# Two layers of attention and feed-forward on one core: third score banks shared between the slots and VectorE, layer one opened in three parts, longer planned loads

## The chip, the cores and the metric

The kernel runs on one core of a Trainium2 chip. The metric is the device time of one execution in microseconds; for the kernel before it is the median of three runs. The profile is of one further execution and shows each engine: PE (TensorE, with its weight loads as PEld), ACT (ScalarE), DVE (VectorE), POOL (GpSimd) and SP, which here only issues transfers.

## The reference

The input is one sequence of 2048 positions with 512 features in bf16. Two equal layers follow one another, each an attention block and a feed-forward block with the same weights in both layers:

```python
def A(x, wqkv, wo):                    # 32 heads of 16
    q, k, v = split(x @ wqkv)
    p = softmax(q @ k.T * 16 ** -0.5)  # 2048 x 2048 for each head
    return (p @ v) @ wo
def B(x, w1, b1, w2, b2):              # 512 -> 1792 -> 512
    return gelu(x @ w1 + b1) @ w2 + b2
for _ in range(2):
    x = x + A(layernorm(x), wqkv, wo)
    x = x + B(layernorm(x), w1, b1, w2, b2)
```

The largest part by count is the exponential of the scores: 2 layers x 32 heads x 2048 x 2048 values.

## The kernel before

**Tiling.** The 2048 queries are cut into four chunks of 512 (the last chunk of layer one into two halves of 256), the keys into 16 tiles of 128, the heads into groups of 8 that share the 128 partitions. A *cell* is the score of one key tile against 512 columns of queries for one quarter of the partitions: a matmul of 32 rows (L1244) that fills one PSUM bank of 128 x 512 float32. There are 4096 cells. A *pass* is one layer, one query chunk, one group and a range of key tiles.

**Two ways to an exponential.** Most cells are read by ACT, which runs exp over two or three neighbouring banks in one instruction and writes bf16 (`exps`, L1601). The others go to DVE: it turns the bank into a 16-bit integer whose bits are an approximate exponential (`dfirst`, L1396), and three more copies of it, shifted by a constant, are made in pairs of cells, one by POOL (L1473), two by DVE (L1478, `dchain`). The value matmul (`pvs`, L1665) then uses one quarter-step for an ACT cell and four for a DVE cell, with scaled copies of V (`vcopies`, L1175), so that the four terms add up to a better exponential. Only the key tiles in `KD` can be DVE cells, five of 16 in each layer.

**Banks.** PSUM has eight banks. Banks 0, 1, 2 are slot 0 and banks 3, 4 slot 1; bank 6 collects the value matmul, of which four run side by side in four column quarters; banks 7 and 5 are `misc`, for projections and feed-forward. Once all first projections of layer zero are through, `grow` takes bank 5 for good and makes it the third bank of slot 1. A score step fills one slot. As it goes out, `swap` may give its third cell to DVE, if DVE is free within half a microsecond; then the slot comes back only when both ACT and DVE have read it (`slot_done`). `attach` may add DVE cells in a free bank of `misc`, and `solo` sends single ones while ACT has long work ahead.

**Parts.** A pass whose key tiles are only some of the 16 leaves its sums in SBUF: after the first part the bank is copied out (L818), and after the last one it is added (L830) and normalised (`norm`). Layer one begins with chunk 0 (8 groups) and half of chunk 1 (4 groups) over key tiles 0 to 11, and then the same 12 passes over tiles 12 to 15. The keys of layer one are ready chunk by chunk, as layer zero's feed-forward (`hpair`, `gelu`, `ytile`) and the projections (`proj`, L556 for all their matmuls) get done beside the attention.

**What sets the order.** All instructions of all engines are put in a fixed order before the launch by a list scheduler (`_Sched`): each operation has a planned cost, a planned latency after which its result counts as there, and a priority; `_Op("sp", cost, ..., tail=...)` is a transfer that holds SP's queue for `cost` and lands `tail` later. On the chip each engine works through its own list in order and waits on semaphores, so a transfer that takes longer than planned holds everything behind its first reader on that engine. Weights come in pieces of 256 KB through a ring of four buffers (`wload`, L933); normalised rows are transposed by DMA (`ln_tile`, L693).

The lines that the change touches most:

```python
SLOTS = ((0, 1, 2), (3, 4))
THIRD = 5
KD = ((4, 5, 6, 7, 8), (0, 1, 2, 12, 13))
...
out += run(1, s0, range(8), most, False, False) + run(1, s1, range(EARLY), most, False, False)
out += run(1, s0, range(8), rest, True, True) + run(1, s1, range(EARLY), rest, True, True)
...
yield _Op("sp", 0.37, lambda e: e.dma_start(dst, src), writes=["WR.%d" % w] + over, sem="dwr%d" % w, by=16, tail=2.48)
```

## Time and profile before

| | us |
|---|---|
| median of three runs (lowest, highest) | 1532.86 (1531.32, 1536.05) |
| profiled execution: its time | 1531.3 |
| profiled execution: its span | 1529.5 |
| ACT busy | 1477.3 |
| PE busy | 1441.2 |
| DVE busy | 1335.0 |
| POOL busy | 821.9 |

The span runs from the first to the last instruction. A row of a group gives the line in the code, the engine, the operation, what is written and read with the shapes, the count, the busy time, the mean duration of one, and the idle time just before them with what ended it. Busy time is counted once where instructions of a group overlap, so for ACT, whose instructions overlap a little, busy time divided by count is what one costs in a row of them. PE's matmuls are pipelined, and its busy time says less about how much more it could do. A row of the waits gives who waited for whom, the total, how often and the longest; PEld rows of that kind are weight loads that wait, often without holding PE.

### The profile page before, as it was taken

How to read it: one execution, taken by the hardware profiler on the slowest of the kernel's cores; microseconds unless marked ns; L12 is line 12 of the kernel's file. 1: busy time of each engine (PE TensorE's matmuls, PEld its weight loads, DVE VectorE, ACT ScalarE, POOL GpSimd, SP SyncE). 2: the span in 40 equal slices, each digit the busy share in tenths (PEclk: the TensorE clock that was granted, in tenths of full speed). 3: DMA queues.
4: the chain of work that ended last, by engine and by line, in shares of the span. 5: the costliest groups of instructions: out<-in, count | busy, mean ns of one | idle time of the engine just before them, and what ended most of it. 6: DMA issues, size and time to landing. Idle time of an engine off the chain costs nothing.

```text
span 1529.5 us, 46372 instructions
## 1 busy us (share of the span) xinstructions
PE 1441.2 (94%) x20257; PEld 441.6 (29%) x20257; DVE 1335.0 (87%) x2259; ACT 1477.3 (97%) x1369; POOL 821.9 (54%) x785
## 2 busy tenths in 40 slices
PE   8998899999999999999999999899999999999998
PEld 3222222222222222222222222222222222334345
DVE  6568889989998999978799778899989989999994
ACT  7999999999999999999999999999999999999995
POOL 5435546655564755545465455567555646464550
PEclk9999999999999999999999999999999999999999
DMA  5100001052111521126121441001143105311523
GB/s 155 41 2 1 2 12 40 29 174 77 48 31 53 144 83 36 43 64 166 50 56 38 130 133 29 1 2 36 37 151 93 43 23 170 109 36 33 167 69 98
DMA packets 145046, 103.40 MB, mean 68 GB/s; under 512 B 37069, under 2 KB 143822, under 8 KB 144846
## 3 DMA queue, kind: packets, MB, share of 16 engines
q1 hardware_dynamic: 144846, 100.44, 23.2%
q8 instruction: 162, 2.65, 0.7%
q14 instruction: 38, 0.31, 0.1%
HBM read 88.61 MB, written 4.19 MB: 61 GB/s over the span
## 4 chain that ended last, share of the span: by engine, by line
ACT 40%; PE 39%; DVE 14%; DMA 5%; POOL 1%; issue 1%; SPq 0%; DVEq 0%; ACTq 0%; POOLq 0%
ACT pt L1601 32%; PE ps L556 13%; PE ps L1665 13%; PE ps L1244 12%; DVE du L1396 6%; DVE du L1478 4%; DMA wr<-in_B_w_dram 2%; ACT kt L1601 2%; ACT q L1601 2%; ACT g L997 2%; DVE g L976 1%; ACT v L1601 1%; POOL xln L689 1%; DMA kt<-in_B_w_dram 1%; DMA xp<-xln 1%
## 5 line engine op out<-in xcount | busy, mean ns | idle before, releaser
L1601 ACT ACTIVATE pt<-ps 128x1024 bf16<-128x1024 f32 (+1 forms) x1112 | 1198.2, 1218 | 19.1 <-PE ps L1244 13.3
L1473 POOL TENSOR_SCALAR du<-du 128x1024 uint16<-128x1024 uint16 (+1 forms) x479 | 562.2, 1175 | 495.6 <-DVE du L1396 481.2
L1396 DVE TENSOR_SCALAR du<-ps 128x512 uint16<-128x512 f32 x956 | 634.9, 680 | 93.5 <-PE ps L1244 88.6
L1244 PE MATMUL ps<-qp,kt 32*128 32x512 bf16 x4096 | 530.0, 384 | 37.3 <-ACT pt L1601 20.7
L1665 PE MATMUL ps<-pt,v 128*17 128x512 bf16 (+1 forms) x2876 | 407.3, 360 | 11.4 <-ACT pt L1601 6.3
L1665 PE MATMUL ps<-du,vc 128*17 128x512 bf16 (+1 forms) x3228 | 384.3, 357 | 3.5 <-ACT pt L1601 1.8
L1478 DVE TENSOR_SCALAR du<-du 128x2048 uint16<-128x2048 uint16 (+1 forms) x479 | 351.4, 743 | 10.7 <-POOL du L1473 10.6
L1244 PEld LDWEIGHTS ps<-qp,kt 32*128 32x128 bf16 x4096 | 137.2, 91 | 581.6 <-ACT pt L1601 214.1
L1665 PE MATMUL ps<-du,v 128*17 128x512 bf16 (+1 forms) x1076 | 178.7, 358 | 10.3 <-ACT pt L1601 3.3
L1673 PE MATMUL ps<-vc,zero 128*17 128x512 bf16 x919 | 182.5, 381 | 0.0
L556 PE MATMUL ps<-xf,wr 128*32 128x512 bf16 (+1 forms) x1888 | 129.5, 364 | 4.2 <-DMA xf<-xln 2.0
L1665 PEld LDWEIGHTS ps<-pt,v 128*17 128x17 bf16 x2876 | 99.2, 88 | 108.0 <-issue 65.2
L1665 PEld LDWEIGHTS ps<-du,vc 128*17 128x17 bf16 x3228 | 100.2, 89 | 89.5 <-issue 54.8
L556 PE MATMUL ps<-wr,g 128*32 128x512 bf16 x1600 | 117.6, 384 | 7.6 <-DMA wr<-in_B_w_dram 6.4
L1192 POOL TENSOR_SCALAR qp<-q,mask 128x512 bf16<-128x512 bf16 (+1 forms) x91 | 71.1, 781 | 76.6 <-PE ps L1244 69.9
L1601 ACT ACTIVATE kt<-ps 128x1536 bf16<-128x1536 f32 (+1 forms) x77 | 98.9, 1294 | 2.9 <-PE ps L1244 1.2
L976 DVE TENSOR_SCALAR g<-ps,hb1t 128x512 bf16<-128x512 f32 (+1 forms) x112 | 78.4, 703 | 6.0 <-PE ps L556 5.4
L1473 POOL TENSOR_SCALAR kt<-kt 128x1024 uint16<-128x1024 uint16 (+1 forms) x46 | 53.4, 1161 | 46.9 <-DVE kt L1396 46.8
L1601 ACT ACTIVATE v<-ps 128x1024 bf16<-128x1024 f32 (+1 forms) x69 | 73.9, 1139 | 2.0 <-PE ps L1244 1.2
L1396 DVE TENSOR_SCALAR kt<-ps 128x512 uint16<-128x512 f32 x91 | 62.0, 681 | 7.3 <-PE ps L1244 5.6
L1665 PE MATMUL ps<-kt,v 128*17 128x512 bf16 (+1 forms) x309 | 67.5, 365 | 0.3 <-ACT pt L1601 0.2
L1665 PEld LDWEIGHTS ps<-du,v 128*17 128x17 bf16 x1076 | 45.1, 88 | 63.3 <-issue 25.7
(90 smaller groups left out, 1234.0 us busy)
## 6 DMA issues: line engine op xcount, KB each, us to landing
wr<-in_B_w_dram SPq DMA_DIRECT2D x256, 256.0 KB, 2.9
wr<-in_A_wqkv_dram SPq DMA_DIRECT2D x24, 256.0 KB, 3.0
wr<-in_A_wo_dram SPq DMA_DIRECT2D x18, 256.0 KB, 3.6
x<-in_A_x_dram SPq DMA_DIRECT2D x7, 512.0 KB, 4.1
kept<-x SPq DMA_DIRECT2D x4, 512.0 KB, 2.9
x<-kept SPq DMA_DIRECT2D x4, 512.0 KB, 3.9
out_dram<-x SPq DMA_DIRECT2D x16, 128.0 KB, 2.4
g<-in_A_wqkv_dram SPq DMA_DIRECT2D x3, 512.0 KB, 5.1
```

The costliest lines, as they stand in the source:

```text
L556: return [lambda e, a=a: e.matmul(out[32 * a:32 * a + 32, :], lhsT=lhsT[:, 32 * a:32 * a + 32], rhs=rhs, start=start, stop=stop, tile_posi ...
L689: yield _Op(eng, cost, lambda e: e.tensor_scalar(T["XLN"][:, x, :], T["X"][:, t % XT, :], T["RSTD"][:, t:t + 1], T["NMR"][:, t:t + 1], op0 ...
L976: yield _Op("dve", 0.21 + n / 966, lambda e, fc=fc, pb=pb: e.tensor_scalar(T["G"][:, fc, q], pb, T["HB1T"][:, fc:fc + 1], None, op0=ALU.ad ...
L997: lambda e, g=g: e.activation(out=g, in_=g, func=ACT.Gelu_apprx_tanh), reads=gk, writes=gk, prio=2)
L1192: yield _Op("pool", 0.27 + 0.42 * w / 512, lambda e, s=s, q=q, i=i, t=t, w=w: e.tensor_scalar(T["QP"][:, s, w * i:w * i + w], q, T["MASK"] ...
L1244: return (lambda e: e.matmul(o, lhsT=lhsT, rhs=rhs, start=True, stop=True, tile_position=(32 * a, 0)), ["K%d.%d.%d" % (l, gb, kt // 4), "Q ...
L1396: yield _Op("dve", 0.682, lambda e: e.tensor_scalar(u, self.bank(b), E_SCALE, E_BIAS, op0=ALU.mult, op1=ALU.add), reads=["B.%d" % b], writ ...
L1473: one = _Op("pool", 0.15 + 0.45 * n, lambda e, a=a, b=b: e.tensor_scalar(b, a, float(SHIFT), 1.0, op0=ALU.add, op1=ALU.mult), reads=key[0] ...
L1478: two = _Op("dve", 0.152 + 0.266 * n, lambda e: e.tensor_scalar(U[:, 2:4, 0:n, :], U[:, 0:2, 0:n, :], 2 * SHIFT, None, op0=ALU.add), reads ...
L1601: yield _Op("act", 0.065 + 0.4267 * n, lambda e, src=src, dst=dst: e.activation(out=dst, in_=src, func=ACT.Exp, scale=0.25), reads=["B.%d" ...
L1665: op.fns.append(lambda e, o=o, lhsT=q[0][0][m], rhs=q[0][1][:, n * m:n * m + n], a=a, st=st, sp=sp: e.matmul(o, lhsT=lhsT, rhs=rhs, start= ...
L1673: op.fns.append(lambda e, o=self.bank(b)[32 * a:32 * a + 17, :], rhs=rhs, a=a, st=not begun[a], sp=end: e.matmul(o, lhsT=T["ZERO"][:, 0:17 ...
```

## The change

- Each slot keeps two banks of its own, 0 and 1, and 3 and 4. Banks 2 and 5 are the slots' thirds and lie in the pool for DVE's cells (`dbank`) while nobody uses them. `grow`, `swap` and `slot_done` go. As a score step goes out, `attach` may put DVE cells into whatever banks are free, the first if DVE is free within half a microsecond, each further one if it is free 0.6 us earlier; if it attached none, `extend` lets ACT's exp take the slot's own third bank, if that is free by then. A slot comes back as soon as ACT has read it. Bank 5 can go to `misc` when more than four operations wait for a bank there, or more than one after the third query chunk of layer one.
- Layer one opens with key tiles 0 to 7, then 8 to 11, then 12 to 15, over the same 12 groups. The middle part is added to the sums in SBUF by DVE. DVE's key tiles in layer one become 0, 1, 2, 8 and 12.
- Planned costs of transfers: weight loads 1.5 and 2.5 in place of 0.37 and 2.48, moves 1.5 and 4.0 in place of 0.42 and 3.7, transposes 0.3 and 3.5 in place of 1.2 and 1.35, stores 1.0 in place of 0.42.
- Smaller ones: the key buffer of chunk 1 of layer one is lent to exp results as those of chunks 3 and 2 are; DVE's reading of a bank goes ahead of its exponent cells where it isn't one; the value matmul goes out with fewer quarters when two (not one) DVE buffers are left; which buffers an instruction is told to wait for is narrowed in three places and widened for the lent ones.

```diff
-SLOTS = ((0, 1, 2), (3, 4))
+SLOTS = ((0, 1), (3, 4))
 PVB = 6
 MISC = (7, 5)
-THIRD = 5
+THIRD = (2, 5)
 PT_RING = 15
-LEND = (3, 2)
+LEND = (3, 2, 1)
...
+DCELL = 0.6
+PARTS = (8, 12)
+KD = ((4, 5, 6, 7, 8), (0, 1, 2, 8, 12))
...
+SEVAC = 0.2
-RUSH = 4
+RUSH = 1
...
-DULOW = 1
+DULOW = 2
...
-LATENCY = {"pe": 0.219, "act": 0.21, "dve": 0.139, "pool": 0.153328, "sp": 0.1}
+LATENCY = {"pe": 0.2185, "act": 0.21, "dve": 0.139, "pool": 0.153328, "sp": 0.1}
...
-                        item.prio = min(th.prio, EVAC)
+                        item.prio = min(th.prio, EVAC if item.writes[0].startswith("DU") else SEVAC)
...
     def xmove(self, c, src, dst, sem, reads, writes):
-        yield _Op("sp", 0.42, lambda e: e.dma_start(dst, src), reads=reads, writes=writes, sem=sem, by=16, tail=3.7)
+        yield _Op("sp", 1.5, lambda e: e.dma_start(dst, src), reads=reads, writes=writes, sem=sem, by=16, tail=4.0)
...
-            yield _Op("sp", 1.2, lambda e: e.dma_start(dst(t), T["XLN"][:, x, :], transpose=True),
-                      reads=["XLN.%d" % x], writes=dkeys(t), sem="dtr%d" % x, by=16, tail=1.35)
+            yield _Op("sp", 0.3, lambda e: e.dma_start(dst(t), T["XLN"][:, x, :], transpose=True),
+                      reads=["XLN.%d" % x], writes=dkeys(t), sem="dtr%d" % x, by=16, tail=3.5)
...
                     yield ("need", ("k1", c))
+                    keys += self.lentkeys(LEND.index(c))
...
-                      writes=["Q.%d.%d" % (i, c)])
+                      writes=["Q.%d.%d" % (i, c)] + (self.lentkeys(len(LEND) + c) if l else []))
...
         if not final:
-            yield _Op("dve", DV, lambda e: e.tensor_copy(pt, pv), reads=[key], writes=[pk] + over)
+            if part:
+                yield _Op("dve", DV, lambda e: e.tensor_tensor(out=pt, in0=pt, in1=pv, op=ALU.add), reads=[key, pk], writes=[pk])
+            else:
+                yield _Op("dve", DV, lambda e: e.tensor_copy(pt, pv), reads=[key], writes=[pk] + over)
...
     def wload(self, piece, src, n, uses, w, over):
         dst = self.T["WR"][w].rearrange("p (c f) -> p c f", c=n)
-        yield _Op("sp", 0.37, lambda e: e.dma_start(dst, src), writes=["WR.%d" % w] + over, sem="dwr%d" % w, by=16, tail=2.48)
+        yield _Op("sp", 1.5, lambda e: e.dma_start(dst, src), writes=["WR.%d" % w] + over, sem="dwr%d" % w, by=16, tail=2.5)
...
-            yield _Op("sp", 0.42, lambda e: e.dma_start(self.hbm["out"][:, t, :], T["X"][:, t % XT, :]), reads=["X.%d" % (t % XT)],
+            yield _Op("sp", 1.0, lambda e: e.dma_start(self.hbm["out"][:, t, :], T["X"][:, t % XT, :]), reads=["X.%d" % (t % XT)],
...
-        every, most, rest = range(NT), range(NT - 4), range(NT - 4, NT)
+        every, parts = range(NT), [range(a, b) for a, b in zip((0,) + PARTS, PARTS + (NT,))]
         self.segs = [[(c, 0, 512) for c in range(self.NQ)] for _ in range(NL)]
         self.segs[-1][-1:] = [(self.NQ - 1, 0, 256), (self.NQ - 1, 256, 256)]
         s0, s1 = self.segs[1][:2]
         out = run(0, s0, range(8), range(4), False, False) + run(0, s0, range(8), range(4, NT), True, True)
         for seg in self.segs[0][1:]:
             out += run(0, seg, range(8), every, False, True)
-        out += run(1, s0, range(8), most, False, False) + run(1, s1, range(EARLY), most, False, False)
-        out += run(1, s0, range(8), rest, True, True) + run(1, s1, range(EARLY), rest, True, True)
+        for i, kts in enumerate(parts):
+            for seg, n in ((s0, 8), (s1, EARLY)):
+                out += run(1, seg, range(n), kts, i > 0, i == len(parts) - 1)
...
+        if b == THIRD[0]:
+            return "misc" if self.ended else "dbank"
         q = self.s.waiting("misc")
         if self.lend == 2:
             return "misc"
...
+        self.fresh = set()
         self.lead = [min(pi for pi, p in enumerate(self.pas) if p[0] == l) for l in range(NL)]
         self.slots = [list(x) for x in SLOTS]
-        self.held, self.users = [len(x) for x in SLOTS], [0] * len(SLOTS)
+        self.held, self.thirds = [len(x) for x in SLOTS], list(THIRD)
         self.dmine = {c for q in self.dlist for c in q}
...
-    def join(self, op, d, b, extra, free):
+    def join(self, op, d, b, extra, free, merge=False):
...
-        if op.fns and not self.third(b):
+        if op.fns and not merge:
             op.after.append(_Op("pe", MM, f, reads=r, writes=["B.%d" % b], mode="S"))
         else:
             op.fns.append(f)
...
-    def swap(self, op, start, cells, extra, free, sl):
-        if extra or self.lend == 2 or len(cells) < 3 or not (self.open or self.s.pools["du"]):
+    def banked(self, b, start):
+        return all(self.s.end.get(ev, 0.0) <= start for ev in self.P.deps([], ["B.%d" % b]) if ev[0] != "pe")
+
+    def extend(self, op, start, cells, extra, free, sl):
+        b, tok = self.thirds[sl], self.s.tokens
+        if extra or len(cells) < 2 or b not in self.s.pools["dbank"] or not self.banked(b, start):
             return
-        if self.s.clock["dve"] > start + SWAP:
+        pa, c = self.pa, self.next_act()
+        if c is None:
             return
-        c = cells[-1]
-        if c in self.dmine:
+        l, seg, g = self.pas[c[0]][:3]
+        need = [("qp", c[0]), ("K", l, self.heads(seg, g)[0], c[1] // 4)]
+        r = []
+        if c[2] not in {x[2] for x in cells} and all(k in tok for k in need):
+            f, r = self.score(c, tok[need[0]], b)
+        if not r or self.s.landed(r) > start:
+            (self.dlist if c in self.dmine else self.alist)[c[0]].insert(0, c)
+            self.pa = pa
             return
-        d = self.next_d({x[2] for x in cells[:-1]}, start)
-        if d is None:
-            return
-        cells.pop()
-        f, r = self.score(c, self.s.tokens[("qp", c[0])], self.slots[sl][2])
-        op.fns.pop()
-        op.writes.pop()
-        self.scored -= 1
-        self.left[c[0]] += 1
-        if self.left[c[0]] == 1:
-            free.remove(self.s.tokens[("qp", c[0])])
-        self.pa = min(self.pa, c[0])
-        self.alist[c[0]].insert(0, c)
-        self.join(op, d, self.slots[sl][2], extra, free)
+        self.s.pools["dbank"].remove(b)
+        cells.append(c)
+        op.fns.append(f)
+        op.reads += r
+        op.writes.append("B.%d" % b)
+        self.take(c, free)
 
...
+                if b in self.thirds and self.s.clock["dve"] + DCELL * len(extra) > start + SWAP:
+                    continue
...
-                self.join(op, d, b, extra, free)
+                self.join(op, d, b, extra, free, self.banked(b, start))
...
-            op.late = lambda op, start, sl=sl, cells=cells, extra=extra, free=free: (self.attach(op, start, cells, extra, free), self.swap(op, start, cells, extra, free, sl))
+            op.late = lambda op, start, sl=sl, cells=cells, extra=extra, free=free: (self.attach(op, start, cells, extra, free), self.extend(op, start, cells, extra, free, sl))
...
-        if not self.third(b):
-            yield ("rel", "dbank", b)
-        else:
-            yield from self.slot_done(self.third(b) - 1)
+        yield ("rel", "dbank", b)
...
-    def third(self, b):
-        return sum(i + 1 for i, x in enumerate(self.slots) if b in x)
-
-    def grow(self):
-        for c in range(self.NQ):
-            for kind in "KVQ":
-                for i in range(4):
-                    yield ("need", (kind, 0, 4 * c + i if kind == "V" else i, c))
-        for home in ("dbank",):
-            yield ("cond", lambda: THIRD in self.s.pools["dbank"] or THIRD in self.s.pools["misc"])
-            home = "dbank" if THIRD in self.s.pools["dbank"] else "misc"
-            yield ("take", (home, THIRD))
-        self.slots[1].append(THIRD)
-
-    def slot_done(self, sl):
-        self.users[sl] -= 1
-        if self.users[sl] == 0:
-            yield ("rel", "s", sl)
-
     def over(self, du):
-        return ["K0.%d.%d" % (i, c) for i in (2, 3) for c in range(self.NQ)] if du == len(self.cap) - 1 else []
+        if du not in self.fresh:
+            return []
+        self.fresh.remove(du)
+        return ["K0.%d.%d" % (i, c) for i in (2, 3) for c in range(self.NQ)]
 
     def morebuf(self):
...
+    def lentkeys(self, b):
+        return ["PT.%d" % u for u in range(*self.blocks[1 + b])]
+
...
-                  writes=["W2.%d" % c] + ["Q.%d.%d" % (i, c) for i in range(NDC)], sem="dw%d" % c, by=16, tail=2.5)
+                  writes=["W2.%d" % c] + ["Q.%d.%d" % (i, c) for i in range(NDC)] + self.lentkeys(len(LEND) + c), sem="dw%d" % c, by=16, tail=2.5)
...
-                reads=["B.%d" % b for b in self.slots[sl][:n]], writes=[k for r in run for k in self.pkeys(r)])
+                reads=["B.%d" % b for b in (self.slots[sl] + self.thirds[sl:sl + 1])[:n]], writes=[k for r in run for k in self.pkeys(r)])
...
-                                         ["V%d.%d" % (l, kt), "V%d1" % l] + self.pkeys(r), ("pt", r), True, kt))
-            yield from self.slot_done(sl)
+                                         ["V%d.%d" % (l, kt), "V%d1" % l, "PT.%d" % r], ("pt", r), True, kt))
+            yield ("rel", "s", sl)
+            if n > 2:
+                yield ("rel", "dbank", self.thirds[sl])
...
-        s.pool("dbank", [])
+        s.pool("dbank", THIRD[:1])
...
-        s.spawn(self.grow(), 0)
```

3 lines of the change are left out of this document (1 added, 2 removed).

## The prediction

> **What bounds the kernel now.** I read the page's engine totals first, then the groups with shapes kept apart, then the windows by stage, the waits, and the load lines one by one.
>
> ```profile
> span 1529.5 us, 46372 instructions
> PE 1441.2 (94%) x20257; PEld 441.6 (29%) x20257; DVE 1335.0 (87%) x2259; ACT 1477.3 (97%) x1369; POOL 821.9 (54%) x785
> ACT 40%; PE 39%; DVE 14%; DMA 5%; POOL 1%; issue 1%; SPq 0%; DVEq 0%; ACTq 0%; POOLq 0%
> ```
>
> ACT is occupied 97% of the span, so only 1529.5 - 1477.3 = 52.2 us can come from filling its gaps; anything more has to take work off ACT. The chain is shared by ACT and PE, so PE cannot be loaded freely either. DVE has the most room: 1529.5 - 1335.0 = 194.5 us idle.
>
> ```profile
> L1601 ACT ACTIVATE pt<-ps 128x1024 bf16<-128x1024 f32 x753 | 735.9, 1072 | 16.1 <-PE ps L1244 12.6 <-PE ps L1665 2.1
> L1601 ACT ACTIVATE pt<-ps 128x1536 bf16<-128x1536 f32 x358 | 511.6, 1526 | 3.0 <-PE ps L1665 1.4 <-PE ps L1244 0.7 <-PE ps L1673 0.6
> L1244 PE MATMUL ps<-qp,kt 32*128 32x512 bf16 x4096 | 530.0, 384 | 37.3 <-ACT pt L1601 20.7 <-DVE du L1396 4.9 <-ACT kt L1601 2.4
> L1396 DVE TENSOR_SCALAR du<-ps 128x512 uint16<-128x512 f32 x956 | 634.9, 680 | 93.5 <-PE ps L1244 88.6
> L1396 DVE TENSOR_SCALAR kt<-ps 128x512 uint16<-128x512 f32 x91 | 62.0, 681 | 7.3 <-PE ps L1244 5.6
> L1478 DVE TENSOR_SCALAR du<-du 128x2048 uint16<-128x2048 uint16 x477 | 350.6, 744 | 10.7 <-POOL du L1473 10.6
> L997 ACT ACTIVATE g<-g 128x3584 bf16<-128x3584 bf16 x14 | 43.9, 3182 | 0.1
> ```
>
> The exp line by itself, one row for each buffer that it writes:
>
> ```profile
> L1601 ACT ACTIVATE pt<-ps x1112: 591/1092/1775, 13.2 to 1499.2; 128x1024 bf16<-128x1024 f32 x116, 128x1536 bf16<-128x1536 f32 x70
> L1601 ACT ACTIVATE kt<-ps x77: 1017/1445/1720, 88.7 to 893.5; 128x1536 bf16<-128x1536 f32 x40, 128x1024 bf16<-128x1024 f32 x37
> L1601 ACT ACTIVATE v<-ps x69: 1017/1069/1520, 1044.0 to 1497.8; 128x1024 bf16<-128x1024 f32 x55, 128x1536 bf16<-128x1536 f32 x14
> L1601 ACT ACTIVATE q<-ps x52: 1017/1112/1633, 261.5 to 1315.8; 128x1024 bf16<-128x1024 f32 x34, 128x1536 bf16<-128x1536 f32 x18
> ```
>
> A cell is one score bank of 512 columns. There are 4096; DVE takes 956 + 91 = 1047 and ACT the other 3049, in 1112 + 77 + 69 + 52 = 1310 exps (the last four rows). Prices from these rows: by busy time divided by count, a two-bank exp occupies ACT for 735.9/753 = 0.977 us and a three-bank one for 511.6/358 = 1.429, so the third bank costs 0.45 us and an instruction as such 0.977 - 2 x 0.452 = 0.073. A cell on DVE costs 0.68 + 0.744/2 = 1.05 us there. So each cell that DVE takes in addition is worth 0.45 us of ACT, and each three-bank exp that falls apart costs 0.073 per instruction more.
>
> **The change, part by part.** First, the third banks. Today banks 2 and 5 belong to their slot: when DVE takes the third cell, the slot is not given back until DVE has read it, and at most one cell per step is swapped to DVE. While ACT runs a gelu (two in a row of 3.2 us in most stages), the slots are full and only bank 7 is left for single DVE cells. The windows of the exponent line on DVE show it, in pairs of a stage before a gelu and the stage with it:
>
> ```profile
> 450.00:475.00 25.00, 13.72 (x22) 1.00 0.11 33
> 475.00:500.00 25.00, 9.86 (x16) 1.00 0.28 85
> 650.00:675.00 25.00, 13.71 (x21) 1.00 0.14 39
> 675.00:700.00 25.00, 6.87 (x10) 0.93 0.45 140
> 825.00:850.00 25.00, 11.99 (x18) 1.00 0.11 33
> 850.00:875.00 25.00, 9.98 (x15) 1.00 0.49 149
> 1075.00:1100.00 25.00, 13.39 (x21) 1.00 0.12 33
> 1100.00:1125.00 25.00, 9.76 (x15) 1.00 0.28 87
> 1375.00:1400.00 25.00, 12.92 (x20) 1.00 0.12 34
> 1400.00:1425.00 25.00, 10.83 (x18) 1.00 0.38 115
> ```
>
> (Columns: stage, its length, DVE busy with that line and how many, granted clock, DMA share, GB/s.) The gelu stages lack 6 + 11 + 3 + 6 + 2 = 28 cells. After the change banks 2 and 5 may be lying free for DVE during a gelu, or may hold a third ACT cell, as it falls; I take half: 14 x 0.45 = **-6.3 us**. The bounds are 0 and 28 x 0.45 = 12.6.
>
> Outside the gelus DVE still waits for scores: 88.6 + 5.6 = 94.2 us in the rows above. The 28 missing cells account for 28 x 1.05 = 29 of it, which leaves 65. An idle DVE can now be given two cells in one step, and a slot need not wait for DVE. I take a third, 22 us, which is 21 cells, 21 x 0.45 = -9.4 us; the bound is 65/1.05 x 0.45 = 28. Against it stands that a third bank used by DVE is missing to its slot's next step, whichever slot the DVE cell came with; then a step carries two cells. How often PE today finds DVE in its way:
>
> ```profile
> PEld ps L1244 <- DVE du L1396: 118.0, 265, 1.3
> ```
>
> In 265 cases a score step waits for a bank that DVE holds. If one in three goes out two wide instead, ACT gets 88 more instructions: 88 x 0.073 = +6.4 us; all 265 would be 19. PE gets 88 more steps; 530.0 us over 1310 steps is 0.40 us a step, so 36 us, covered by PE's 1529.5 - 1441.2 = 88 us idle. If that cover is gone, they cost up to 36. Net of this part **-3.0 us**, between -28 and +19. The Trainium skill, page "ScalarE: Activation LUTs", section "What ACT_TABLE_LOAD costs", speaks against this step more than my row: it gives an ACTIVATE with immediates 186 ns beside its elements, of which about 93 overlap with its neighbour, so 93 ns a piece. By it the 88 instructions would cost an estimated 8.2 us, and the whole forecast would be 1.8 us later.
>
> Second, the loads. The plan counted a weight load as 0.37 us of the queue and 2.48 to landing, and now counts 1.5 and 2.5; moves, transposes and stores are stretched too. The load line itself, the waits on it over the whole run, and ACT's two gaps in the worst stage:
>
> ```profile
> L933 SPq DMA_DIRECT2D wr<-in_B_w_dram x256: 367/368/1429, 10.1 to 1506.8; - x128
> DMA to landing us min/median/max: 2.5/3.0/5.9
> PEld ps L556 <- DMA wr<-in_B_w_dram: 12.0, 19, 1.4
> PE ps L556 <- DMA wr<-in_B_w_dram: 6.4, 8, 1.1
> 687.97 1.02 ACT L1601 ACTIVATE pt<-ps 128x1024 bf16<-128x1024 f32 x1 [0.84 <-PE ps L1244]
> 689.91 1.02 ACT L1601 ACTIVATE pt<-ps 128x1024 bf16<-128x1024 f32 x1 [0.92 <-PE ps L1244]
> ```
>
> Issue goes from 0.37 to 1.43 us, and landing to 5.9, so the old figure is the best case and the new one near the worst. PE runs a fixed order: a late weight holds the scores behind it, and ACT and DVE after them. PE waits 12.0 + 6.4 = 18.4 us on these weights. In the stage 675 to 700 ACT lost 0.84 + 0.92 = 1.8 us behind it. Between 0 and 18.4 I take **-3.4 us**, two such stages, since most waits are short and ACT has one slot in hand. Nothing is issued more often; SP's queue keeps the same loads (256 in the row above), and only the matmuls that use them are put later. A chunk's 28 second-layer loads planned 1.13 us slower each end 32 us later at most; that is hidden while nothing downstream is due, and would cost up to 32 us where it is.
>
> Third, layer one opens with key tiles 0-7, then 8-11, then 12-15, so chunk 2 of its keys is due 192 cells later than now. ACT's gaps around that opening, and the prices of one more part:
>
> ```profile
> 745.06 5.13 ACT L1601 ACTIVATE pt<-ps 128x1024 bf16<-128x1024 f32 x5 [0.66 <-PE ps L1244]
> 757.26 2.79 ACT L1601 ACTIVATE pt<-ps 128x1536 bf16<-128x1536 f32 x2 [0.71 <-PE ps L1244]
> 791.85 6.46 ACT L1601 ACTIVATE pt<-ps 128x1024 bf16<-128x1024 f32 x6 [1.88 <-PE ps L1665]
> 866.31 2.14 ACT L1601 ACTIVATE kt<-ps 128x1024 bf16<-128x1024 f32 x2 [0.70 <-PE ps L1244]
> L830 DVE TENSOR_TENSOR v<-v,ps x16: 670/677/689, 98.9 to 1023.0; 128x512 f32<-128x512 f32 x16
> L1192 POOL TENSOR_SCALAR qp<-q,mask 128x512 bf16<-128x512 bf16 x75 | 60.7, 809 | 67.3 <-PE ps L1244 61.0 <-ACT q L756 5.7
> PE ps L1665 <- DVE v L830: 3.7, 10, 0.8
> ```
>
> The four gaps are 0.66 + 0.71 + 1.88 + 0.70 = 4.0 us; I take 2.7 back (bounds 0 and 4.0). Twelve more passes mean 12 additions on DVE, 12 x 0.677 = 8.1 us, or 7.7 cells not taken, 3.5 us of ACT if DVE were full; it is not in this stretch, so half, +1.7. They mean 12 x 0.81 = 9.7 us on POOL, queued between its shifts for DVE, covered by POOL's 46% idle; without that cover each would delay a DVE pair by 0.8. Each boundary also keeps the single accumulator bank from PE for about 0.37 us (3.7/10), 4.4 us under PE's idle time, or all of it on the path. Net **-1.0 us**, from -4.0 to +8.
>
> The rest I put at 0 together, with ends of -3 and +5. Evacuations ahead of DVE's cells free bank 7 sooner and make a DVE cell wait one instruction of 0.68. Lending bank 5 to the projections (over four waiters, over one near the end) narrows slot 1 meanwhile. Four more tile units for exps help a ring on which ACT shows no wait; the key evacuations and the late weight load that now also wait for these units come long after the units were read. Offering vectors at two free buffers sends out emptier accumulation steps, on PE's idle time. The last 30 us, after the final exp, run as before.
>
> Sum: -6.3 - 3.0 - 3.4 - 1.0 = **-13.7 us**. The profiled execution took 1531.3 us (span 1529.5); it lies 1.6 under the median 1532.86 of the three runs. Applied to the median it gives **1519 us**.
>
> **The rivals.** (A) Two-cell steps make PE the bound, slower than before. DVE picks the third bank that has been free longest, so a cell of slot 1's step can sit in bank 2, and both slots then lose a third in turn. For it: the chain gives PE 39%, and some stages have no PE room at all:
>
> ```profile
> 1150.00:1175.00 25.00, 25.00 (x334) 6.82 (x330) 24.64 (x42) 25.00 (x27) 15.18 (x14) 1.00 0.35 106
> 1175.00:1200.00 25.00, 22.93 (x307) 6.31 (x304) 23.19 (x42) 25.00 (x22) 17.00 (x16) 1.00 0.19 44
> ```
>
> (Here PE, weight load, DVE, ACT and POOL.) Against: the stage beside it has 2 us of room in 25. From about 88/0.40 = 220 extra steps PE's idle time is used up; at 250, with half of them in full stages, 125 x 0.40 = 50 us are added, less the 6.3 + 3.4 = 9.7 us of the gelu stages and the loads, which makes about 1573 (ACT's 250 x 0.073 = 18 us lie beside it). Milder, at 150 steps with a third exposed, 20 - 9.7 = +10, **1543**, which I take as this rival's time. (B) The plan only shifts: DVE takes as many cells as now, and the loads' -3.4 is all that is left beside the boundaries' +1.7: **1531**. For it: DVE's own supply, 5 of 16 key tiles, is not raised. (C) The longer planned loads put the feed-forward work off into the layer's opening, where the 32 us above are due at once: half exposed, 16, less the banks' 6.3 + 3.0, makes +6.7: **1540**. Against: the same opening is relaxed by 192 cells.
>
> **How the numbers follow.** Forecast (1504 to 1527) 0.67, A 0.13, B 0.10, C 0.10. A measurement of this kernel tells about 0.3%, 4.6 us, from no change: its three runs span 1531.32 to 1536.05. B lies within it; A and C are slower. So faster 0.67, same 0.10, slower 0.23. The likeliest case's own range goes from -29, a little under half of what all gains' bounds give together (12.6 + 28 + 18.4 + 4.0 + 3 = 66; ACT, PE and DVE cannot all be relieved at once), to -6, where the floating banks cost 3 outside the gelus in place of gaining 3 and the loads give half: 1504 to 1527. For 8 in 10 I leave out the far ends of A and of the gains: 1503 to 1547.
>
> **What would show it.** DVE's exponent line should count 1070 to 1100 cells instead of 1047, with the gelu stages at 15 or more; two-bank exps some 90 up; PE's waits on weights below 10 us; 12 additions more and ACT's gaps around the opening under 2 us; ACT busy near 1465. It would be wrong if the exps rise by 150 or more with DVE's count unchanged (A), if DVE's count stays within 10 (B), or if ACT shows gaps of microseconds where layer one opens (C).

## The result and the profile after

| | before | after |
|---|---|---|
| median (lowest, highest), four runs each | 1534.45 (1531.32, 1537.68) | 1513.76 (1513.23, 1514.69) |
| profiled execution (one of the four): its time | 1531.3 | 1514.7 |
| its span | 1529.5 | 1512.9 |
| ACT busy, and idle in the span | 1477.3, 52.2 | 1475.2, 37.7 |

The ratio is 0.9866, with a 95% interval from 0.9842 to 0.9889: the change made the kernel faster by 1.3%, 20.7 us by these medians and 16.6 by the two profiled executions. (Why these two differ is told under the clock, below.) The forecast was 1519.

The engine totals and the head of the chain of waits of the changed kernel:

```profile
span 1512.9 us, 46350 instructions
PE 1455.4 (96%) x20161; PEld 439.5 (29%) x20161; DVE 1364.8 (90%) x2295; ACT 1475.2 (98%) x1433; POOL 844.0 (56%) x811
ACT 55%; PE 29%; DVE 13%; DMA 1%; POOL 1%; issue 1%; ACTq 0%
```

The split of the gain stands in the first two lines. The span is 16.6 us shorter, but ACT is busy only 2.1 us less; the other 14.5 us are gaps of ACT that closed. In the chain ACT's share rose from 40% to 55%, and DMA's fell from 5% to 1%. Next, the groups of ACT whose gaps changed, with all shapes of a buffer in one row (the last columns are busy time and mean, then the idle time before them and its releasers); first the kernel before:

```profile
L1601 ACT ACTIVATE pt<-ps 128x1024 bf16<-128x1024 f32 (+1 forms) x1112 | 1198.2, 1218 | 19.1 <-PE ps L1244 13.3 <-PE ps L1665 3.6 <-PE ps L1673 0.6
L1601 ACT ACTIVATE kt<-ps 128x1536 bf16<-128x1536 f32 (+1 forms) x77 | 98.9, 1294 | 2.9 <-PE ps L1244 1.2 <-PE ps L1665 0.8
L1601 ACT ACTIVATE v<-ps 128x1024 bf16<-128x1024 f32 (+1 forms) x69 | 73.9, 1139 | 2.0 <-PE ps L1244 1.2 <-PE ps L1673 0.2
L1601 ACT ACTIVATE q<-ps 128x1024 bf16<-128x1024 f32 (+1 forms) x52 | 61.3, 1206 | 0.8 <-PE ps L1244 0.6
L971 ACT ACTIVATE g<-ps,hb1t 128x256 bf16<-128x256 f32 x14 | 6.0, 474 | 4.3 <-PE ps L556 4.3
```

and the kernel after:

```profile
L1601 ACT ACTIVATE pt<-ps 128x1024 bf16<-128x1024 f32 (+1 forms) x1111 | 1144.3, 1160 | 8.3 <-PE ps L1667 5.0 <-PE ps L1255 2.4
L1601 ACT ACTIVATE kt<-ps 128x1024 bf16<-128x1024 f32 (+1 forms) x126 | 145.4, 1178 | 3.1 <-PE ps L1255 1.3
L1601 ACT ACTIVATE v<-ps 128x1024 bf16<-128x1024 f32 (+1 forms) x89 | 97.3, 1143 | 1.0
L1601 ACT ACTIVATE q<-ps 128x1024 bf16<-128x1024 f32 (+1 forms) x48 | 56.0, 1213 | 0.4 <-PE ps L1255 0.3
L978 ACT ACTIVATE g<-ps,hb1t 128x256 bf16<-128x256 f32 x14 | 6.0, 473 | 1.2 <-PE ps L559 1.2
```

The exps waited 19.1 + 2.9 + 2.0 + 0.8 = 24.8 us before and 8.3 + 3.1 + 1.0 + 0.4 = 12.8 after; the waits for scores (L1244, now L1255) fell from 16.3 to 4.0 us (13.3 + 1.2 + 1.2 + 0.6 against 2.4 + 1.3 + 0.3). The small gelus near the end, which read a bank directly (L971, now L978), gave 3.1 more. The counts say how the work changed: 1111 + 126 + 89 + 48 = 1374 exps in place of 1310, so 64 more instructions. The main buffer's exps by shape:

```profile
L1601 ACT ACTIVATE pt<-ps 128x1024 bf16<-128x1024 f32 x883 | 852.7, 1073 | 2.1 <-PE ps L1255 1.4
L1601 ACT ACTIVATE pt<-ps 128x1536 bf16<-128x1536 f32 x228 | 328.3, 1499 | 6.2 <-PE ps L1667 5.0 <-PE ps L1255 1.1
```

They were 753 and 358 before. Over all four buffers two-bank exps rose from 879 to 1083, and three-bank ones fell from 430 to 291. And the lines of DVE that matter, by shape (L1411 was L1396, L1475 was L1478; L823 is the new addition, which has 4 more in another buffer):

```profile
L1411 DVE TENSOR_SCALAR du<-ps 128x512 uint16<-128x512 f32 x967 | 632.9, 682 | 61.8 <-PE ps L1255 57.7
L1411 DVE TENSOR_SCALAR kt<-ps 128x512 uint16<-128x512 f32 x90 | 59.8, 682 | 5.6 <-PE ps L1255 5.5
L1475 DVE TENSOR_SCALAR du<-du 128x2048 uint16<-128x2048 uint16 x475 | 358.4, 769 | 8.3 <-POOL du L1470 8.2
L1475 DVE TENSOR_SCALAR du<-du 128x1024 uint16<-128x1024 uint16 x17 | 8.5, 511 | 0.5 <-POOL du L1470 0.5
L823 DVE TENSOR_TENSOR v<-v,ps 128x512 f32<-128x512 f32 x8 | 5.4, 680 | 0.2 <-PE ps L1667 0.2
```

DVE takes 967 + 90 = 1057 cells, only 10 more than before. At 0.45 us that is 4.5 us less for ACT, and 64 instructions at 0.073 are 4.7 more: ACT's work is nearly the same, as its busy time says. DVE's waits for scores did fall, from 94.2 to 57.7 + 5.5 = 63.2 us, but the freed time did not go into cells. DVE is busy 1364.8 - 1335.0 = 29.8 us more, and half of that is the copies of a DVE cell in this buffer: 358.4 + 8.5 us, where the kernel before has 350.6 for 477 long ones and 0.8 for two short ones. There are two fewer long copies, but each takes longer (769 ns in place of 744), and 15 more short ones. Why the long ones take longer no run shows. With the twelve new additions (12 x 0.68 = 8.2) that is some 23 us.

The stages of the gelus, 20 us each from the table load ahead of the pair, DVE's exponent line alone (length, busy and count, granted clock, DMA share, GB/s); before:

```profile
299.16:319.16 20.00, 9.89 (x15) 1.00 0.47 145
484.56:504.56 20.00, 8.41 (x13) 1.00 0.43 132
674.54:694.54 20.00, 5.50 (x8) 0.91 0.37 117
845.76:865.76 20.00, 6.07 (x9) 1.00 0.48 144
1110.42:1130.42 20.00, 9.16 (x15) 1.00 0.52 158
1242.78:1262.78 20.00, 7.48 (x11) 1.00 0.05 15
1405.01:1425.01 20.00, 9.21 (x15) 1.00 0.48 143
```

and after:

```profile
300.01:320.01 20.00, 8.74 (x14) 1.00 0.47 140
485.33:505.33 20.00, 9.10 (x14) 1.00 0.51 146
662.39:682.39 20.00, 7.88 (x12) 1.00 0.50 145
843.75:863.75 20.00, 11.07 (x17) 1.00 0.49 146
1101.66:1121.66 20.00, 9.44 (x15) 1.00 0.47 135
1245.07:1265.07 20.00, 10.44 (x16) 1.00 0.44 130
1383.47:1403.47 20.00, 9.78 (x15) 1.00 0.45 134
```

The counts add to 86 before and 103 after: 17 more cells at the gelus, so about 7 fewer everywhere else. Most of them are only taken at another time: from 10 us ahead of each table load to 30 us behind it, the same line counts 200 cells before and 206 after. The third row of before shows something else too, a granted clock of 0.91; no stage after has that.

Last, PE's waits on feed-forward weights, 18.4 us before, and after:

```profile
PEld ps L559 <- DMA wr<-in_B_w_dram: 2.0, 3, 0.8
PE ps L559 <- DMA wr<-in_B_w_dram: 0.5, 2, 0.3
```

The loads themselves, by the load line:

```profile
L940 SPq DMA_DIRECT2D wr<-in_B_w_dram x256: 367/368/1813, 9.7 to 1491.2; - x128
DMA to landing us min/median/max: 2.5/2.9/5.9
```

The loads themselves are as slow as they were (up to 1.81 us to issue, 1.43 before, and up to 5.9 to land in both). It is the order that differs: PE seldom comes to a weight before it has landed.

### The profile page after: what moved, and what is told of

It reads as the page before. It is cut to its first block, busy times and chain, and to the rows that moved or that the text cites. A ratio compares the mean times of both kernels' runs of the same rounds, so it can differ in the third digit from the quotient of the medians.

```text
span 1512.9 us, 46350 instructions
## 1 busy us (share of the span) xinstructions
PE 1455.4 (96%) x20161; PEld 439.5 (29%) x20161; DVE 1364.8 (90%) x2295; ACT 1475.2 (98%) x1433; POOL 844.0 (56%) x811
## 4 chain that ended last, share of the span: by engine, by line
ACT 55%; PE 29%; DVE 13%; DMA 1%; POOL 1%; issue 1%; ACTq 0%
ACT pt L1601 39%; PE ps L559 10%; PE ps L1255 9%; PE ps L1667 9%; ACT kt L1601 6%; DVE du L1411 6%; ACT v L1601 3%; DVE du L1475 3%; ACT g L1004 3%; ACT q L1601 2%; DMA xf<-xln 1%; ACT L1004 1%; ACT L1601 1%; DVE kt L1411 1%; DVE stats L669 1%
## 5 line engine op out<-in xcount | busy, mean ns | idle before, releaser
L1601 ACT ACTIVATE pt<-ps 128x1024 bf16<-128x1024 f32 (+1 forms) x1111 | 1144.3, 1160 | 8.3 <-PE ps L1667 5.0
L1411 DVE TENSOR_SCALAR du<-ps 128x512 uint16<-128x512 f32 x967 | 632.9, 682 | 61.8 <-PE ps L1255 57.7
L1255 PE MATMUL ps<-qp,kt 32*128 32x512 bf16 x4096 | 551.1, 384 | 27.2 <-ACT pt L1601 14.9
L1667 PE MATMUL ps<-du,vc 128*17 128x512 bf16 (+1 forms) x3243 | 400.1, 358 | 3.6 <-POOL du L1470 1.1
L1667 PE MATMUL ps<-pt,v 128*17 128x512 bf16 (+1 forms) x2706 | 395.8, 361 | 5.6 <-ACT pt L1601 3.1
L1475 DVE TENSOR_SCALAR du<-du 128x2048 uint16<-128x2048 uint16 (+1 forms) x492 | 366.4, 760 | 8.8 <-POOL du L1470 8.7
L1255 PEld LDWEIGHTS ps<-qp,kt 32*128 32x128 bf16 x4096 | 144.1, 91 | 591.4 <-ACT pt L1601 188.8
L1675 PE MATMUL ps<-vc,zero 128*17 128x512 bf16 x1109 | 208.5, 381 | 0.0
L1601 ACT ACTIVATE kt<-ps 128x1024 bf16<-128x1024 f32 (+1 forms) x126 | 145.4, 1178 | 3.1 <-PE ps L1255 1.3
L1203 POOL TENSOR_SCALAR qp<-q,mask 128x512 bf16<-128x512 bf16 (+1 forms) x103 | 83.4, 810 | 48.0 <-PE ps L1255 41.3
L1601 ACT ACTIVATE v<-ps 128x1024 bf16<-128x1024 f32 (+1 forms) x89 | 97.3, 1143 | 1.0
L1667 PE MATMUL ps<-kt,v 128*17 128x512 bf16 (+1 forms) x395 | 93.7, 369 | 0.7 <-ACT pt L1601 0.3
L1411 DVE TENSOR_SCALAR kt<-ps 128x512 uint16<-128x512 f32 x90 | 59.8, 682 | 5.6 <-PE ps L1255 5.5
```

Of the source, the lines that this page charges most:

```text
L1203: yield _Op("pool", 0.27 + 0.42 * w / 512, lambda e, s=s, q=q, i=i, t=t, w=w: e.tensor_scalar(T["QP"][:, s, w * i:w * i + w], q, T["MASK"] ...
L1255: return (lambda e: e.matmul(o, lhsT=lhsT, rhs=rhs, start=True, stop=True, tile_position=(32 * a, 0)), ["K%d.%d.%d" % (l, gb, kt // 4), "Q ...
L1411: yield _Op("dve", 0.682, lambda e: e.tensor_scalar(u, self.bank(b), E_SCALE, E_BIAS, op0=ALU.mult, op1=ALU.add), reads=["B.%d" % b], writ ...
L1475: two = _Op("dve", 0.152 + 0.266 * n, lambda e: e.tensor_scalar(U[:, 2:4, 0:n, :], U[:, 0:2, 0:n, :], 2 * SHIFT, None, op0=ALU.add), reads ...
L1601: yield _Op("act", 0.065 + 0.4267 * n, lambda e, src=src, dst=dst: e.activation(out=dst, in_=src, func=ACT.Exp, scale=0.25), reads=["B.%d" ...
L1667: op.fns.append(lambda e, o=o, lhsT=q[0][0][m], rhs=q[0][1][:, n * m:n * m + n], a=a, st=st, sp=sp: e.matmul(o, lhsT=lhsT, rhs=rhs, start= ...
```

## The experiments

The questions: did the time come from the loads, from the banks or from the three parts, and are 20 us more than what another order would bring by chance? In the list below each comparison is with runs of the kernel before on the same chip. The variants marked * have their own planned latency of PE (0.2165 to 0.2195 us, as their expectations say); what that alone does was measured too.

| kernel | median (lowest, highest) | ratio to before [95%] |
|---|---|---|
| before, order kept, short weight loads | 1523.80 (1522.19, 1527.30) | 0.9940 [0.9921, 0.9960] |
| loads alone * | 1520.82 (1520.41, 1521.47) | 0.9922 [0.9896, 0.9948] |
| floating banks alone * | 1520.27 (1519.49, 1524.00) | 0.9928 [0.9907, 0.9950] |
| parts alone * | 1536.61 (1531.99, 1542.63) | 1.0041 [1.0024, 1.0057] |
| loads and parts * | 1523.36 (1522.65, 1523.94) | 0.9943 [0.9925, 0.9961] |
| loads and floating banks * | 1521.23 (1520.29, 1522.11) | 0.9930 [0.9911, 0.9948] |
| floating banks and parts * | 1516.60 (1516.10, 1518.82) | 0.9897 [0.9870, 0.9924] |
| after once more | 1512.82 (1512.32, 1513.91) | 0.9883 [0.9868, 0.9899] |
| after, order kept, short weight loads | 1512.97 (1512.42, 1514.13) | 0.9877 [0.9855, 0.9899] |
| after, another constant | 1517.94 (1517.80, 1518.57) | 0.9903 [0.9872, 0.9933] |
| before, another constant | 1536.20 (1534.38, 1538.88) | 1.0036 [1.0022, 1.0050] |
| after, middle planned loads * | 1511.65 (1511.15, 1512.59) | 0.9876 [0.9857, 0.9894] |

**Weights that are never late, order of before.**

```diff
         dst = self.T["WR"][w].rearrange("p (c f) -> p c f", c=n)
+        if w in self.wfull:
+            dst, src = dst[0:16], src[0:16]
...
+        self.wfull |= {w} - set(range(W_RING, W_RING + W_MORE))
```

After the first load of each of the four ring buffers, the kernel leaves out 112 of the 128 partitions of every weight load.

> The kernel before with its order of work unchanged; after the first load of each of the four ring buffers every weight load brings only 16 of its 128 partitions, so that it lands earlier (the rest of the weights stays what it was, so the numbers computed are not the reference's). Theory S (most of the gain is that PE no longer stands at weights that land later than planned): PE's waits on weights fall from 18.4 us to under 5, ACT's gaps before exps fall from 21.5 us to about 10, and the time falls by 8 to 14 us. Theory K (the gain comes from the floating third banks): the gaps stay above 17 us and the time falls by at most 4 us.

Measured: 1523.8, 0.6% under before (6 to 12 us by the interval), with the same instructions in the same order. PE's waits on these weights are nearly gone:

```profile
PEld ps L556 <- DMA wr<-in_B_w_dram: 0.9, 2, 0.6
```

So the late weights cost the kernel before about 9 us, half of what the whole change brings. (Shorter loads also leave other transfers more room; but PE's waits for normalised rows did not fall by it: 4.6 us before, 5.6 here.) That part of the theory of late loads is right. What it said of ACT's gaps was not seen: in the profiled execution exps still wait 13.4 us for scores in their main buffer. But that execution was the slowest of the six (1527.3), with two stretches at half clock; the first is shown at the end.

**The same in the order of after.** The same edit in the changed kernel:

> The changed kernel with its order unchanged and the weight loads shortened as in the run on the kernel before (16 of 128 partitions after the first load of each ring buffer; weights otherwise stay what they were, so the numbers computed are not the reference's). Theory S: nothing is left to win, it is faster by at most 1.5 us; on the kernel before the same edit gave 0.994 of its time. If loads still hold PE in the changed kernel, it gains 3 us or more.

Measured: 1512.97, against 1513.76 and 1512.82 for the changed kernel itself. So these weights have nothing left to give. With them out of both orders, 1523.8 - 1513.0 = 10.8 us remain (9.7 by the ratios), which are not these weights. Late normalised rows are among them: PE waits 5.6 us for rows in the first and 1.1 in the second.

**Longer planned loads alone.** In the kernel before, the new costs of weight loads, moves, transposes and stores, and nothing else:

```diff
-        yield _Op("sp", 0.37, ..., by=16, tail=2.48)
+        yield _Op("sp", 1.5, ..., by=16, tail=2.5)
```

> The kernel before with the new planned costs of all transfers alone, PE's planned latency 0.2175 (again the value whose plan is shortest). Theory S: PE's waits on weights under 5 us, ACT's gaps before exps about 9 to 12 us, time 8 to 14 us under the kernel before, near 1522. Theory K: within 4 us of the kernel before.

Measured: 0.9922, some 12 us.

```profile
PE 1447.3 (95%) x20337; PEld 445.9 (29%) x20337; DVE 1332.7 (88%) x2255; ACT 1476.9 (97%) x1374; POOL 826.2 (54%) x783
ACT 58%; PE 29%; DVE 10%; issue 1%; POOL 1%; DMA 0%; ACTq 0%; DVEq 0%
```

ACT's and DVE's work are those of before, and DMA has left the chain: the span of 1519.6 is shorter through gaps alone (ACT idle 42.7 in place of 52.2). The list of waits has none of PE on these weights any more. The time is what the theory of late loads said; its mark for ACT's gaps before exps, 9 to 12 us, was missed: by the same rows of waits they are 15.2 us, against 21.5.

**All but the loads.** The changed kernel with the old planned costs:

```diff
-        yield _Op("sp", 1.5, ..., by=16, tail=2.5)
+        yield _Op("sp", 0.37, ..., by=16, tail=2.48)
```

> The changed kernel with the old planned costs of all transfers, and PE's planned latency 0.217 instead of 0.2185, the value of that constant at which this variant's order comes out shortest in the plan. Floating banks and three parts stay. Theory S: PE's waits on weights come back to 15 us or more, ACT's gaps before exps to 18 to 24 us, and the kernel is 8 to 14 us slower than the changed one, near 1525. Theory K: within 4 us of the changed kernel.

Measured: 1516.6, only 3 to 4 us above the changed kernel. The theory of late loads, which put most of the gain there, misses; the theory of the banks holds as to the time. PE waits on weights again, but little:

```profile
PEld ps L559 <- DMA wr<-in_B_w_dram: 5.9, 14, 0.9
PE ps L559 <- DMA wr<-in_B_w_dram: 1.3, 4, 0.4
```

7.2 us, where the kernel before has 18.4 with the same planned loads. So the new order has most of its weights in time without having planned for it. The next run shows that this comes with the floating banks.

**Floating banks alone.** The changed kernel with old loads and with layer one in two parts (key tiles 0 to 11, then the rest, and DVE's key tiles of before):

```diff
-PARTS = (8, 12)
-KD = ((4, 5, 6, 7, 8), (0, 1, 2, 8, 12))
+PARTS = (12,)
+KD = ((4, 5, 6, 7, 8), (0, 1, 2, 12, 13))
```

> The floating third banks alone, with the smaller edits: the changed kernel with the old planned transfers and two parts; planned latency of PE 0.2175. Theory S: PE's waits on weights are back at 15 us or more and the kernel gains under 5 us on the one before. Theory K: it gains 8 to 14 us, 1519 to 1525, by more DVE cells (about 1060) and by ACT's gaps, although weights still come late.

Measured: 0.9928, some 11 us, as much as the loads alone. The engine totals, and PE's waits on weights:

```profile
PE 1455.5 (96%) x20168; PEld 440.8 (29%) x20168; DVE 1350.2 (89%) x2286; ACT 1473.5 (97%) x1443; POOL 843.4 (56%) x797
```

```profile
PEld ps L559 <- DMA wr<-in_B_w_dram: 5.8, 12, 1.1
PE ps L559 <- DMA wr<-in_B_w_dram: 0.6, 1, 0.6
```

In its span of 1517.7 ACT is idle for 44.2 us in place of 52.2 and busy for 3.8 less: here too most of it is gaps. The exps' wait for scores in their main buffer is 6.0 us, 13.3 in the kernel before. DVE takes 1062 cells, 15 more. But PE's waits on weights fell as well, to 6.4 us, although the loads are planned as in the kernel before, which has 18.4 (the third part alone, below, has 23.7). So a part of what the floating banks bring may be weights that are no longer late. How large a part, and how the banks do it, is open: the short loads were not run with this kernel. That it is not all of it is shown by the two kernels with short loads, which are still 10 us apart, though by banks, parts and the other transfers together.

**All but the floating banks.** The kernel before with the new loads and the three parts:

> The kernel before with the new planned transfers and the three parts, but with its own fixed third banks and the swap; planned latency of PE 0.2165. Theory S (late loads are most of it): within 3 us of the changed kernel. Theory K (the floating banks carry a share beside the loads): 1518 to 1523, as the loads alone gave 1520.8, with some 1040 DVE cells and 1315 exps.

Measured: 1523.36, just above the range of the theory of the banks. With the floating banks on top the changed kernel is 9.6 us (by 1513.76) faster.

**All but the third part.** The changed kernel with the edit of the floating banks above, but with the new loads:

> The changed kernel with layer one opened in two parts again (key tiles 0 to 11, then 12 to 15, and the old key tiles for DVE), planned latency of PE 0.2165, the value whose plan is shortest. If the three parts carry a share of the gain, as my prediction had it only by 1 us net, ACT's gaps around 740 to 900 us come back by 2 to 4 us and the kernel is 3 to 8 us slower than the changed one, 1517 to 1522. If they carry nothing, it stays within 2 us.

Measured: 1521.23, so the third part is worth 7.5 us here; the prediction had 1.0.

```profile
PE 1457.6 (96%) x20198; PEld 443.7 (29%) x20198; DVE 1346.3 (89%) x2261; ACT 1480.9 (97%) x1431; POOL 829.1 (55%) x788
```

ACT is busy 5.7 us more than after, and DVE takes 1046 cells instead of 1057: 11 cells x 0.45 = 5.0 us. ACT's idle time is only 1.7 us more (39.4 against 37.7). So the third part pays by cells for DVE more than by gaps. Its own boundary and the move of DVE's key tile from 13 to 8 were always changed together, so which of the two does it stays open.

**The third part alone.** The kernel before with `PARTS = (8, 12)` and the new key tiles:

> The kernel before with the three parts of layer one alone (banks and planned transfers as before; planned latency of PE 0.2165, the value whose plan is shortest). Theory U: 1520 to 1526 like the other edits alone. Theory S+K, with the parts worth some 3 to 7 us only together with the floating banks: 1528 to 1536.

Measured: 1.0041, slower, with 23.7 us of waits on weights (16.1 + 7.6). In the profiled execution, which lies near the median, ACT is busy for 1482.2 us, 4.9 more than before, as DVE takes only 1038 cells; its idle time is that of before (52.5). Part of the loss is the clock (below), but there is no gain. On top of the loads, too, the third part costs 2.5 us (1523.4 against 1520.8; that is less than a planned constant moves, below). It gains only beside the floating banks.

**How much an order is worth by itself.** The same program with one planned constant moved, in the changed kernel from 0.2185 to 0.219 and in the kernel before from 0.219 to 0.2215:

```diff
-LATENCY = {"pe": 0.2185, "act": 0.21, ...
+LATENCY = {"pe": 0.219, "act": 0.21, ...
```

> The changed kernel with PE's planned latency at 0.219 us, the value before, in place of 0.2185: nothing but that constant. Theory P (the order of work reacts to any small constant, and some of the gain is which order happened to come out): the time moves by 4 to 12 us, most likely up, with ACT's gaps as in the changed kernel and a different count of DVE cells or exps. If the order is robust, it stays within 3 us.

> The kernel before with PE's planned latency at 0.2215 us in place of 0.219 and nothing else, which gives another order (1042 DVE cells, 1304 exps). Loads alone, floating banks alone and even late-load relief alone each gave 9 to 13 us, which together is far more than the 20 us of the whole change. Theory U (the order of the kernel before is an unlucky one on the chip, and any other order gains much of this): 1520 to 1526, with ACT's gaps before exps of 8 to 14 us. Theory S+K (each edit earns its gain): within 4 us of the kernel before, with PE's waits on weights still above 12 us and ACT's gaps near 20.

Measured: the changed kernel loses 4.2 us by half a nanosecond of planned latency, and the kernel before 5.5 us (0.36%). The theory that the order of before was merely an unlucky one finds no support: the two other orders tried with its banks and its planned loads, this one and the third part alone, are slower still (with the constant, PE waits 24.1 us on weights). But single comparisons above carry some 4 to 6 us of this kind, so gains of 10 are safe and their digits are not.

```profile
ACT pt L1601 <- PE ps L1667: 11.4, 7, 3.2
```

With 0.219 ACT waits 11.4 us for scores behind value matmuls, in 7 places, where it is 5.0 us in the changed kernel: 6.4 us from the order alone. ACT is even busy 5.4 us less there (1469.8), as DVE takes 1067 cells; its idle time is 8.8 us more.

**A version that is a little faster.** The changed kernel with planned weight loads of 1.0 in place of 1.5, transposes landing after 2.6 in place of 3.5, and the constant 0.2195; beside it the changed kernel itself:

> The changed kernel with transfers planned between median and upper end: weight loads 1.0 us of the queue in place of 1.5, transposes 2.6 to landing in place of 3.5, PE's planned latency 0.2195. If the plan of the changed kernel gives away more than it needs, this is 2 to 5 us faster, near 1510, with PE's waits on weights at 2 to 6 us. If the upper end is needed, those waits rise over 8 us and it is 2 to 6 us slower.

> The changed kernel itself, on the chip of the other runs of this call, as their measure: 0.9866 of the time before within 0.003, 1512 to 1516 us.

Measured: 1511.65 (1511.15 to 1512.59) against 1512.82 (1512.32 to 1513.91) on the same chip. It is the fastest of all, but by 1.2 us, less than a constant moves and less than the 2 to 5 expected. PE's waits on weights are 0.9 us, so the longer figures were not needed to keep them low.

**What the set says together.** By the ratios, loads alone bring 12 us, floating banks alone 11, and both without the third part 10.7: in time they overlap almost wholly. In gaps they overlap less: ACT is idle 9.5 us less with the loads, 8.0 with the banks and 12.8 with both. With both, though, DVE takes 1046 cells in place of the 1062 with the banks alone, and ACT is busy 7.4 us more (16 x 0.45 = 7.2). Why that order leaves DVE fewer cells is open. The third part costs 6 alone, costs 2.5 on the loads, and gives 4 to 8 beside the floating banks (1520.3 - 1516.6 = 3.7 with the old loads, 1521.2 - 1513.8 = 7.5 with the new ones). All three bring 18 to 20.

## Why the prediction was right, and where it was wrong

The time (1519 against 1513.8, inside 1503 to 1547 and also inside the narrower 1504 to 1527) and the sign were right. The sum that gave them was not: it took 7.6 us from ACT's work (6.3 + 3.0, less 1.7 for the additions) and 6.1 from its gaps (3.4 + 2.7), and 2.1 came from work and 14.5 from gaps. The total came near because 5.5 us too much of the one nearly made up for 8.4 too little of the other; that is luck. Of its marks, PE's waits on weights (2.5 us) and the 12 additions came true; DVE's cells (1057, not 1070 to 1100), the two-bank exps (204 more, not some 90) and ACT's busy time (1475.2, not near 1465, which its own sum did not give either: 1477.3 - 7.6 = 1469.7) did not.

- **Gelu stages, -6.3.** Right for the stages themselves: 14 cells forecast, 17 measured, 17 x 0.45 = 7.7 us. Four of the seven stages reach the mark of 15 in 20 us, and two lack one cell. But in the 40 us around each pair only 6 cells remain, 2.7 us: most of the 17 were shifted and not added, and the step did not ask where they would come from.
- **Floating banks elsewhere, -3.0.** This step failed. "I take a third, 22 us, which is 21 cells": DVE's wait for scores fell by 31 us, more than assumed, but outside the gelus it took 7 cells fewer, while copies and additions filled 23 us. The 88 more instructions came near (64), by luck: the step took one more instruction for each exp that falls back to two banks, and 139 of them did, but the cells left over filled further two-bank exps. By the step's own prices, the 7 cells and the 64 instructions cost 7 x 0.45 + 4.7 = 7.9 us, where it had a gain of 3.0. (The Trainium skill's page "ScalarE: Activation LUTs", section "What ACT_TABLE_LOAD costs", would make the instructions an estimated 64 x 0.093 = 6.0; ACT's busy time came out 2.1 lower than before, under both sums, and nearer the smaller price.) The step priced banks by cells, and they pay by gaps: with the floating banks alone, ACT's idle time fell by 8.0 us. That this is the slot that no longer waits for DVE is not shown: the row `PEld ps L1255 <- DVE du L1411`, loads of score steps that wait for DVE to read a bank, has 132.8 us in 307 places with the floating banks alone, against 118.0 us in 265 before, and it does not say whether the bank is wanted for an exp or for a DVE cell. The weights that come in time (6.4 us of waits in place of 18.4) are another reading. Which of the change's bank rules does it was not tried apart.
- **Loads, -3.4.** The mechanism was right, the size not: about 9 us with only the lateness taken away, 12 with the new planned costs alone. The cover, "ACT has one slot in hand", did not hold: more than twice the 3.4 us came back. As the last step, on top of banks and parts, the loads bring 3 to 4, so the number came near only because the other steps had taken most of it, and that was not the reason given.
- **Three parts, -1.0.** Mis-sized, 7.5 beside the others, and for another reason. Between 730 and 880 us, where the four gaps of the prediction lie, ACT's idle time fell from 5.2 to 2.8 us, near the 2.7 forecast, though not under 2; but without the third part it is 1.9, so the third part is not what closed them. (Chunk 2 of the keys is also due later than the 192 cells of the prediction: by the order of the passes it was due after the first 32 cells, and now after 12 x 32 = 384.) The largest gaps of the opening in the changed kernel are

```profile
797.96 9.21 ACT L1601 ACTIVATE pt<-ps 128x1536 bf16<-128x1536 f32 x9 [1.42 <-PE ps L1667]
1009.59 3.28 ACT L1601 ACTIVATE pt<-ps 128x1536 bf16<-128x1536 f32 x3 [1.61 <-PE ps L1667]
```

  which are 3.0 us for two, the second near the end of the opening. The 12 additions came as forecast.
- **Rivals.** (A), PE as the bound, did not come: 64 more steps, not 150, and PE is busy 96%. (C) did not come: no gap above 1.7 us at the opening. (B) said that DVE's count would stay within 10 and the time at 1531: the count did stay within 10, and the time fell all the same. As a mark it did not tell the cases apart, because it saw only one of ACT's two sources of time.

## What to carry to other kernels

Where an engine is busy 97% and a fixed order feeds it, price a change by the gaps that it closes as well as by the work that it takes away, and read afterwards, from busy time against span, which of the two moved. Steps that remove the same gap do not add up, and one that costs alone may pay beside another, so a set of them is measured with each left out and each alone. Before a few us are put down to an edit, move a constant that means nothing by a hair and see what the order alone does.

## What the runs showed of the hardware

**Half-clock stretches after short stalls, and the spread of the runs.** I had not expected that PE's clock falls behind loads that are 1 us late. TensorE's granted clock in the kernel before, in steps of 2 us (PE busy and count, clock, DMA share, GB/s):

```profile
684.00:686.00 2.00, 0.94 (x11) 1.00 0.86 274
686.00:688.00 2.00, 1.52 (x19) 0.78 0.60 195
688.00:690.00 2.00, 2.00 (x19) 0.50 0.46 143
690.00:692.00 2.00, 2.00 (x26) 0.87 0.38 131
```

The lost share is 0.22 x 2 + 0.50 x 2 + 0.13 x 2 = 1.7 us, as of 3.4 us at half clock. It is the only such stretch of that execution between 16 and 1506 us. It follows two waits of PE on weights, 0.94 and 1.11 us, 2 us apart:

```profile
684.43 0.61 PE L556 MATMUL ps<-wr,g 128*32 128x512 bf16 x8 [0.94 <-DMA wr<-in_B_w_dram]
686.48 0.61 PE L556 MATMUL ps<-wr,g 128*32 128x512 bf16 x8 [1.11 <-DMA wr<-in_B_w_dram]
```

The kernel before with short weight loads has two such stretches in its profiled execution, each behind a normalised row that was late; here the first, and the wait in it:

```profile
362.00:364.00 2.00, 0.58 (x14) 1.00 0.74 265
364.00:366.00 2.00, 2.00 (x22) 0.58 0.15 26
366.00:368.00 2.00, 2.00 (x19) 0.57 0.68 238
```

```profile
363.43 0.62 PE L556 MATMUL ps<-xp,wr 128*32 128x512 bf16 x8 [1.42 <-DMA xp<-xln]
```

A wait as long does not always bring one. The kernel before waits 1.62 us for a row at 1481 us, and the kernel with the floating banks alone 1.99 us at 1348; in both the clock stays at 1.00 in the 6 us behind. So what decides is not the length of one wait, and it stays open.

The Trainium skill, page "TensorE: Matmul & The Clock Gate", section "What's actually happening", has the length, a window of 3413 ns, and a half-rate state; but it has that state follow an idle window of about 3.4 us. Here PE idled for 1 to 2 us within 4, less than such a window, and the measurement decides.

Each run's mean granted clock goes with the time of the runs of the kernel before, 30 beside the experiments:

```
mean clock   runs   median us   lowest to highest
1.000          8    1529.72     1529.01 to 1530.41
0.999         10    1530.54     1528.57 to 1533.26
0.998          7    1534.88     1532.88 to 1535.15
0.997          4    1534.82     1532.71 to 1538.27
0.995          1    1536.10
```

A straight line through the 30 gives 1.75 us for each 0.001 of clock, where 0.001 of the span is 1.5 us. So most of the 10 us between its runs goes with the clock, as a few such stretches would make it (1.7 us is 0.0011 of the span); how many each run had is seen in the profiled ones alone. All 8 runs of the changed kernel show 1.000 and lie within 2.4 us. At a clock of 1.000 on both sides the gain is about 1529.7 - 1513.3 = 16.4 us, near the difference of the profiled spans; the other 1 to 4 us of the medians go with the clock of the kernel before. The runs of the third part alone go from 1532.0 at 0.999 to 1542.6 at 0.994, so its spread is of this kind too. In its profiled execution two such stretches cost 3.4 us, 1.7 more than before, beside the 4.9 us that ACT is busy more. In the kernel before with short weight loads the three runs at 1.000 take 1522.2 to 1523.9: so 7 of its 9 us are not the clock.

That a stall of PE is the cause of a stretch, and not only what comes ahead of it, was not tried by itself.
